# Two FFT convolution layers, twice: PSUM tiles that take any idle buffer, modal convolutions under the planner, mode rows loaded without a cast

## The chip, the cores and the metric

One core of a Trainium2 chip runs the whole program; the times are microseconds of that core. [...] The engines work on SBUF, on PSUM (eight banks, into which PE writes its products) and through DMA on the memory outside. Each engine takes its queue in order; semaphores hold an instruction until what it needs is there.

## The reference

Two layers alternate, twice, on a sequence of 2048 positions and 512 channels, in single precision:

```python
def _A_ref(q, k, v, shift_k, ssm_k, ssm_D):
    ...                                   # k_shift: causal convolution of k over 4 positions
    kv = k_shift * v
    kv_f, kf_f = rfft2(kv padded to 4096), rfft2(ssm_k padded to 4096)
    y = irfft2(kv_f * kf_f)[:, :S, :] + kv * ssm_D[None, None, :]
    return q * y

def _B_ref(u, log_A_real, A_imag, C_real, C_imag, log_dt, D_skip):
    A = -jnp.exp(log_A_real) + 1j * A_imag          # 128 modes for each channel
    C = (C_real + 1j * C_imag) * dt[:, None]
    P = jnp.exp((A * dt[:, None])[:, :, None] * pos[None, None, :])
    K = 2.0 * jnp.einsum("dn,dnl->dl", C, P).real   # 2048 taps from the modes
    y = irfft(rfft(u) * rfft(K))[:, :, :L] + u * D_skip
    return y

x = x + _A_ref(_layernorm(x), ...)
x = x + _B_ref(_layernorm(x), ...)
x = x + _A_ref(_layernorm(x), ...)
x = x + _B_ref(_layernorm(x), ...)
```

The convolution inside A and the taps K do not depend on `x`. So both are worked out once; the second A layer only scales a stored result.

## The kernel before

The program has four parts.

1. *Preparation.* The mode parameters are turned into logarithms and phases on 128 x 512 tiles. `split` (lines 627 to 634) writes each as a rounded value (a cast on ACT) and the rest (a subtraction, `hl[:, 1] = v - hl[:, 0]`, on the engine that it is given), and stores both to `rows_d`. Four tiles are split: `la` and `ai` on POOL, `ph` and `t2` on DVE.
2. *The long stage*, two streams that share the engines. `stream` builds the taps of layer B: `load_rows` (line 720) fetches the rows of a group of channels, `mags` multiplies them with tables (`pm`) and takes the exponential on ACT (`m`), `angles` puts phases into `pa`, rounds them on DVE (`y`) and subtracts the rounding by a second matmul into the same `pa`, `waves` takes sines on ACT, `products` multiplies on POOL (`xy`) and DVE (`e`), `contract` sums on PE (`pk`); there are 64 such steps, 4 for each of the 16 groups. When 4 groups are done, `spectrum_quarter` transforms their taps and stores the spectrum (`pc` to `spec`). `diagonal` works out the products of layer A (`kvt`, `prod`, `kv`), the spectrum of its kernel, the convolution of all four quarters of the channels, and updates `x`. A convolution is a chain: a forward transform in two steps (`pf`, then DVE transposes to `z`, then `pu`), products with the stored spectrum `kab` (`vv`, `sw`), an inverse transform in two steps (`pi`, a copy to `ie` by ACT, DVE transposes to `w`, then `po`), and `finish`.
3. *First modal round*: the normalization of `x`, and `conv_b(0)`. Here ACT writes the normalized `u` and copies `pu` into `sw`, POOL multiplies `sw` with `kab`, DVE writes `vv`.
4. *The scaling by the stored second A layer* (`gated_update`) and the *second modal round*, `conv_b(1)`, during which `x<-x,off` (`restore`, line 1085) puts back the mean on DVE.

*What sets the order.* Every operation goes through `Planner.record`. While `deferred` is false it is issued at once, in the order of the program (these rows bear line 177). While it is true, `flush` issues the operations in the order of `Planner.plan` (rows with line 342): a list schedule, which takes next the operation that can start first by given costs, with the order of recording between equals. In `plan` a tile is ready when the tile that was in its buffer has no reader left: `self.prior` gives each tile the one that many places earlier in its tag's rotation as there are buffers. Preparation, both modal rounds and the scaling are issued at once; only the long stage is planned, up to line 986. DVE and POOL exclude each other in the plan for operations with two SBUF inputs.

*PSUM.* During the long stage `f1` has two buffers of two banks, for `pf`, `pu`, `pi` and `pm`; `c1` has one bank for `kv` and `po`; `pa` has two banks and `pk` one. In the modal rounds `f1` has three buffers and `c1` two.

Of the kernel before, what the change touches and what calls it, by code (L numbers as in the profile page):

```python
# [102 lines left out]
class Op:  # L103
    def __init__(self, engine, n):
        self.engine, self.n, self.calls, self.uses, self.before, self.ordered = engine, n, [], [], set(), []
        self.ins = None


class Planner:
    RELEASE = {"V": 34, "S": 60, "G": 90, "T": 80, "D": 27}  # L110

    def __init__(self, tc, nc):
        self.tc, self.ops, self.tiles, self.deferred = tc, [], {}, False
# [106 lines left out]
    def prepare(self):  # L220
        ops = self.ops
        self.costs = [self.cost(op) for op in ops]
        self.follow = [[] for _ in ops]
# [5 lines left out]
        self.pending = [len(op.before) + len(op.ordered) for op in ops]  # L229
        names, self.prior, self.queue = {}, [], {}  # L230
        self.using, self.users = [], []
        for op in ops:
            l = []
            for t in op.uses:
                if t.tag_meta is None:
                    continue
                if t.name not in names:
                    names[t.name] = len(self.prior)
                    q = self.queue.setdefault(t.tag, [])
                    self.prior.append(q[-t.tag_meta.bufs] if len(q) >= t.tag_meta.bufs else None)  # L240
                    q.append(len(self.prior) - 1)
                    self.users.append(0)
                l.append(names[t.name])
                self.users[names[t.name]] += 1
            self.using.append(l)

    def plan(self, rank=None):
# [3 lines left out]
        idle, live = [0.0] * len(prior), [False] * len(prior)  # L251
        free = dict.fromkeys(self.engines, 0.0)
        ready = [0.0] * len(ops)
        start, end = [0.0] * len(ops), [0.0] * len(ops)
# [6 lines left out]
        for waiting in range(len(ops)):  # L261
            best = None
            for e, l in avail.items():
                pick = None
                base = free[e]
                if e == "D":
                    base = max(base, min(lanes))
                for n in l:
                    t = max(base, ready[n])
                    if e in "VG" and costs[n][2]:  # L270
                        t = max(t, lock["G" if e == "V" else "V"])
                    if pick is not None and (t, rank[n]) >= pick[:2]:
# [18 lines left out]
            op = ops[n]  # L291
            avail[e].remove(n)
            for u in using[n]:
                live[u] = True
            o, lat, extra = costs[n]
            start[n] = t
# [16 lines left out]
            if op.calls[0][0] == "dma_start":  # L313
                server = max(server, t + o) + extra
                end[n] = max(t + o + 1500, server + 1200)
                if e == "D":
                    lanes[lanes.index(min(lanes))] = end[n]
            elif e in "VG" and extra:
                lock[e] = t + o
            for u in using[n]:  # L320
                left[u] -= 1
                idle[u] = max(idle[u], end[n])
            for f, real in self.follow[n]:
                pending[f] -= 1
                ready[f] = max(ready[f], end[n] + self.RELEASE[ops[f].engine] if real else start[n] + o)
                if not pending[f]:
                    avail[ops[f].engine].append(f)
        self.length = max(end)
# [2 lines left out]
    def best(self):  # L331
        return self.plan()

    def flush(self):
        last = {}
        self.prepare()
        for n in self.best():
            op = self.ops[n]
            if op.ins is not None:
                continue  # L340
            for i, (name, a, k) in enumerate(op.calls):
                ins = getattr(self.engines[op.engine], name)(*a, **k).ins  # L342
# [11 lines left out]
def kernel(ctx: ExitStack, tc: tile.TileContext, out, x_in, kv_in, ssmk_in, ssmd_in,  # L354
                           la_in, ai_in, cr_in, ci_in, ldt_in, ldtb_in, dsk_in,
                           w1_in, w2_in, mm_in, w4_in, minus_in, tt_in, tg1_in, tg2_in, dbg=None):
    nc = tc.nc
    planner = Planner(tc, nc)
    V, S, G, T, Q = [planner.engine(e) for e in "VSGTD"]
    after = planner.after  # L360

# [497 lines left out]
    with ExitStack() as actx:  # L859
# [300 lines left out]
    G.tensor_sub(nbs[1], nb, nbs[1])  # L1160
    for _ in conv_b(1):
        pass


def run_steps(gens):
# [62 lines left out]
```

## Time and profile before

| | |
|---|---|
| median of 3 runs | 748.78 us (744.72 to 751.23) |
| the profiled execution | 749.08 us, of which the span from first to last instruction 747.2 us |
| busy: PE, DVE, ACT, POOL | 553.5, 508.5, 404.9, 350.1 us |
| transfers | 138.97 MB, 186 GB/s on average |

A timeline row gives the start, the length, the engine, the line, the operation, output <- inputs, the shapes and the count of instructions merged; in brackets stands the time for which the engine was idle before it and what ended that. A row of a stretch gives its bounds and length, the busy time of PE, PEld, DVE, ACT and POOL, PE's granted clock, the busy share of the transfer engines and GB/s.

### The profile page before, as it was taken

What the parts mean: (1) busy time and instruction counts of PE and PEld (TensorE: products, weight loads), DVE (VectorE), ACT (ScalarE), POOL (GpSimd) and SP (SyncE); (2) the same over time, 40 slices, a digit from 0 to 9 for tenths busy, and PEclk for the clock granted to TensorE, in tenths of its full rate; (3) what the DMA queues carried; (4) which work ended last, traced back from release to release, by engine and by line L of the source; (5) the groups of instructions that cost most, each with busy time, mean ns of one, the idle gap of its engine ahead of it and who ended that gap; (6) DMA issues with size and microseconds to landing.
All of it is one profiled execution on the core that took longest, in us unless ns stands there. A gap on an engine that the chain in (4) does not pass through costs nothing. (4 is left out here: it accounts for less than half of the span.)

```text
span 747.2 us, 20838 instructions
## 1 busy us (share of the span) xinstructions
PE 553.5 (74%) x8568; PEld 307.6 (41%) x8568; DVE 508.5 (68%) x918; ACT 404.9 (54%) x768; POOL 350.1 (47%) x342
## 2 busy tenths in 40 slices
PE   1649688896798888798778789344798871589984
PEld 0114334333334434664354366122465530255662
DVE  6924965547653456578978659664588879978863
ACT  4118518655539878749445386237473326746341
POOL 3618866967756745432353053500554520254551
PEclk9988979998989659698897979876899995899998
DMA  9499858694465315565676745679686712068764
GB/s 245 121 228 236 260 153 237 182 245 125 130 197 181 132 50 150 180 210 163 199 191 232 226 124 182 171 253 277 200 283 228 253 66 104 2 212 261 250 207 93
DMA packets 74499, 138.97 MB, mean 186 GB/s; under 512 B 8092, under 2 KB 37156, under 8 KB 72356
## 3 DMA queue, kind: packets, MB, share of 16 engines
q1 hardware_dynamic: 73540, 135.21, 60.7%
q0 software_dynamic: 864, 2.43, 0.9%
q8 instruction: 68, 1.11, 0.6%
q14 instruction: 27, 0.22, 0.1%
HBM read 97.75 MB, written 39.85 MB: 184 GB/s over the span
## 5 line engine op out<-in xcount | busy, mean ns | idle before, releaser
L342 POOL TENSOR_TENSOR xy<-tt,m 128x512 f32<-128x512 f32 x128 | 148.5, 1185 | 143.9 <-ACT tt L342 64.0
L177 POOL TENSOR_TENSOR sw<-sw,kab 128x512 f32<-128x512 f32 x64 | 80.6, 1280 | 119.3 <-ACT sw L177 112.1
L342 PE MATMUL kv<-prod,minus 128*128 128x512 f32 x128 | 80.3, 720 | 9.3 <-DVE prod L342 7.1
L342 POOL TENSOR_TENSOR prod<-kvt 128x512 f32<-128x512 f32 x64 | 79.8, 1269 | 15.6 <-DMA kv_d<-prod 9.7
L342 ACT ACTIVATE m<-pm 128x1024 f32<-128x1024 f32 x48 | 46.9, 1026 | 57.8 <-PE pm L342 55.9
L342 PE MATMUL pf<-kk,w 64*128 64x512 f32 x128 | 45.0, 755 | 39.9 <-DMA kk<-ssmk_in 21.0
L342 ACT ACTIVATE ab<-pa 128x512 f32<-128x512 f32 x64 | 38.3, 599 | 61.0 <-PE pa L342 61.0
L342 DVE TENSOR_TENSOR e<-pa,m 128x512 f32<-128x512 f32 x64 | 43.6, 681 | 31.5 <-ACT pa L342 25.3
L177 DVE TENSOR_TENSOR vv<-pu,kab 128x512 f32<-128x512 f32 x64 | 40.9, 677 | 35.0 <-ACT sw L177 32.5
L177 ACT COPY ie<-pi 128x1024 f32<-128x1024 f32 x32 | 32.4, 1013 | 58.7 <-PE pi L177 58.7
L342 DVE TENSOR_SCALAR y<-pa 128x512 fp32r<-128x512 f32 x64 | 43.5, 682 | 30.0 <-PE pa L342 29.5
L177 PE MATMUL pf<-u,w 64*128 64x512 f32 (+1 forms) x136 | 40.1, 681 | 25.8 <-ACT u L177 15.8
L342 DVE STREAM_TRANSPOSE zk<-pf 128x512 f32<-128x512 f32 x64 | 41.4, 688 | 25.1 <-PE pf L342 25.1
L177 PE MATMUL pi<-vv,mm 64*64 64x128 f32 x1024 | 53.4, 276 | 1.1 <-DVE vv L177 1.1
L177 PE MATMUL pi<-sw,mm 64*64 64x128 f32 x1024 | 52.3, 270 | 1.7 <-issue 1.7
L342 PE MATMUL pa<-tt,rw 64*128 64x512 f32 x64 | 35.2, 554 | 23.1 <-DVE e L342 23.0
L342 PE MATMUL pa<-y,minus 128*128 128x512 f32 x64 | 41.9, 660 | 10.1 <-DVE y L342 10.1
L342 PE MATMUL pk<-xy,e 128*32 128x64 f32 x2048 | 47.3, 240 | 2.9 <-POOL xy L342 1.5
L177 ACT COPY sw<-pu 128x1024 f32<-128x1024 f32 x32 | 32.3, 1013 | 30.7 <-PE pu L177 30.7
L177 PE MATMUL pu<-zu,w 64*64 64x128 f32 x1024 | 37.2, 281 | 14.3 <-DVE zu L177 12.2
L342 PEld LDWEIGHTS pk<-xy,e 128*32 128x32 f32 x2048 | 36.0, 121 | 28.6 <-issue 19.8
L342 PE MATMUL pu<-zk,w 64*64 64x128 f32 x1024 | 40.0, 301 | 9.3 <-DVE zk L342 6.6
(134 smaller groups left out, 1181.1 us busy)
## 6 DMA issues: line engine op xcount, KB each, us to landing
kab<-spec SPq DMA_DIRECT2D x94, 512.0 KB, 4.6
spec<-pc SPq DMA_DIRECT2D x64, 256.0 KB, 4.3
kvt<-kv_in SPq DMA_DIRECT2D x32, 312.0 KB, 5.0
kk<-ssmk_in SPq DMA_DIRECT2D x32, 128.0 KB, 5.7
xr<-x_in SPq DMA_DIRECT2D x8, 512.0 KB, 6.6
kv_d<-prod SPq DMA_DIRECT2D x16, 256.0 KB, 3.9
kdram<-ks SPq DMA_DIRECT2D x64, 64.0 KB, 2.2
kk<-kdram SPq DMA_DIRECT2D x32, 128.0 KB, 2.8
```

What stands on the lines that cost most here:

```text
L177: op.ins = getattr(self.engines[key], name)(*a, **k).ins
L342: ins = getattr(self.engines[op.engine], name)(*a, **k).ins
```

## The change

- In `plan`, tiles of the tags `c1` and `f1` of the long stage's PSUM pool (`shared`) have no place in a rotation: when an operation is chosen, its tile gets any buffer of the tag that is idle. `flush` moves the operands onto that buffer's first tile (so rows of the change show `pf` for all tiles of `f1`, and `kv` for all of `c1`). The tags of the modal rounds keep their rotation.
- The modal rounds and the scaling are planned too: the first flush comes after the first 16 steps of `conv_b(0)`, and a second one plans the rest. Since pools `xp` and `conv_q` lie where `conv_a` was, operations on them wait in the plan until all that use `conv_a` are done (`over`).
- `load_rows` loads straight into the matmul operand `rw`, four buffers instead of two and two; the cast goes.
- The second matmul of each `pm` is held in the plan until 600 ns ahead of the end of the last sine (`late`).
- The subtractions of `split(1, ...)` and `split(3, ...)` go to POOL.

```diff
 def prepare(self):
...
+                    pool = next((p for p in self.over if f"_{p}_" in t.tag), None)
+                    self.gate.append(self.over.get(pool))
                     q = self.queue.setdefault(t.tag, [])
-                    self.prior.append(q[-t.tag_meta.bufs] if len(q) >= t.tag_meta.bufs else None)
+                    ring = self.name(t) not in self.shared
+                    self.prior.append(q[-t.tag_meta.bufs] if ring and len(q) >= t.tag_meta.bufs else None)
+                    self.tag.append(None if ring else t.tag)
...
 def plan(self, rank=None):
...
                     for u in using[n]:
-                        if live[u] or prior[u] is None:
+                        if live[u]:
+                            continue
+                        if self.gate[u]:
+                            if rest[self.gate[u]]:
+                                ok = False
+                                break
+                            t = max(t, last[self.gate[u]] + self.RELEASE[e])
+                        tag = self.tag[u]
+                        if tag:
+                            if not open_[tag] or (self.FIFO and self.queue[tag][head[tag]] != u):
+                                ok = False
+                                break
+                            t = max(t, min(spare[tag][b] for b in open_[tag]) + self.RELEASE[e])
+                            continue
+                        if prior[u] is None:
                             continue
...
+                if tag and not live[u]:
+                    fit = [b for b in open_[tag] if spare[tag][b] + self.RELEASE[e] <= t + 1e-6]
+                    self.place[u] = max(fit, key=lambda b: (spare[tag][b], -b))
+                    open_[tag].remove(self.place[u])
...
+    planner.over = {"xp": "conv_a", "conv_q": "conv_a"}
+    planner.shared = {'c1_ps', 'f1_ps'}
...
-    split(1, ph, V)
-    split(3, t2, V)
+    split(1, ph, G)
+    split(3, t2, G)
...
-        raw = wk.tile([128, 2, 128], F32, name="raw", tag="raw", bufs=2)
+        rows[gi] = wk.tile([128, 2, 128], F32R, name="rw", tag="rw", bufs=4)
         q, g = divmod(gi, 4)
         for k in range(2):
-            Q.dma_start(raw[:, k, :], rows_d[k][q, :, g, :])
-        rows[gi] = wk.tile([128, 2, 128], F32R, name="rw", tag="rw", bufs=2)
-        V.tensor_copy(rows[gi], raw)
+            Q.dma_start(rows[gi].bitcast(F32)[:, k, :], rows_d[k][q, :, g, :])
...
-            T.matmul(pm[:, h], rows[gi][hs, 1, :], rhs, start=True, stop=True)
+            ins = T.matmul(pm[:, h], rows[gi][hs, 1, :], rhs, start=True, stop=True)
+            if last_sin[0] is not None and h:
+                ins.late.append((last_sin[0], 600))
...
         run_steps([(stream(), RT), (diag, RD)])
-        planner.flush()
...
     for _ in range(2 * NCH):
         next(first)
+    planner.flush()
     gctx.close()
     pctx.close()
+    planner.deferred = True
...
     for _ in conv_b(1):
         pass
+    planner.flush()
```

The order of the instructions changes on every engine. Three places follow; a row is one or more like instructions of an engine's queue.

PE, in the long stage, around the thirtieth of the 64 steps of the taps (`pa<-tt,rw` is its first matmul, `pa<-y,minus` the second, which needs DVE's `y`). Before:

```order
L342 MATMUL pu<-zk,w_108 64x128 x32
L342 MATMUL pk<-xy,e_625 32x64 x16
L342 MATMUL pa<-tt,rw 128x512
L342 MATMUL pa<-y,minus 128x512
L342 MATMUL pa<-tt,rw 128x512
L342 MATMUL pk<-xy,e_631 32x64 x16
L342 MATMUL pa<-y,minus 128x512
```

And in the change, at the same step:

```order
L411 MATMUL pk<-xy,e_616 32x64 x16
L411 MATMUL pa<-tt,rw 128x512
L411 MATMUL pf<-zk,w_108 64x128 x16
L411 MATMUL pa<-tt,rw 128x512
L411 MATMUL pk<-xy,e_622 32x64 x16
L411 MATMUL pa<-y,minus 128x512
L411 MATMUL pf<-kk,w_107 128x16x16x2 x2
```

The second matmul of the step stood directly behind the first; now 16 matmuls of another tile, a further first matmul and 16 of `pk` lie between. In the whole list the two stand side by side 9 times before and 3 times in the change. At the end of the stage both lists have the last `pk`, `pf`, `pu` and `po` in turn.

ACT, at the start of the first modal round (`u` is the normalized input, `sw` a copy of the transformed one). Before:

```order
L177 ACTIVATE u<-x,nb,rs 128x128 x40
L177 COPY sw<-pu 128x1024 x3
L177 COPY ie<-pi 128x64x16
L177 COPY sw<-pu 128x1024
L177 COPY ie<-pi 128x64x16
```

And in the change:

```order
L411 ACTIVATE u<-x,nb,rs 128x128 x31
L411 COPY sw<-pu 128x1024
L411 ACTIVATE u<-x,nb,rs 128x128 x6
L411 COPY sw<-pu 128x1024
L411 ACTIVATE u<-x,nb,rs 128x128 x3
L411 COPY sw<-pu 128x1024
L411 COPY ie<-pi 128x64x16
```

The first copy moved ahead of nine of the forty `u`, the second ahead of three. Over both rounds, in 7 of the 32 pairs of `vv` one half now stands ahead of ACT's copy of the same `pu`; before it was none.

DVE, at the start of the second modal round (`zu` are transposes of the first transform, `x<-x,off` puts back the mean). Before:

```order
L177 STREAM_TRANSPOSE zu<-pf 128x512 x4
L177 TENSOR_SCALAR x<-x,off 128x512 x4
L177 STREAM_TRANSPOSE zu<-pf 128x512 x2
L177 TENSOR_SCALAR x<-x,off 128x512 x4
L177 STREAM_TRANSPOSE zu<-pf 128x512 x2
L177 TENSOR_SCALAR x<-x,off 128x512 x8
L177 TENSOR_TENSOR vv<-pu,kab 128x512 x2
```

And in the change:

```order
L411 TENSOR_SCALAR x<-x,off 128x512 x4
L411 STREAM_TRANSPOSE zu<-pf 128x512 x8
L411 TENSOR_SCALAR x<-x,off 128x512
L411 STREAM_TRANSPOSE zu<-pf 128x512 x2
L411 TENSOR_SCALAR x<-x,off 128x512 x2
L411 TENSOR_TENSOR vv<-pu,kab 128x512 x2
L411 TENSOR_SCALAR x<-x,off 128x512 x2
L411 TENSOR_TENSOR vv<-pu,kab 128x512 x2
L411 STREAM_TRANSPOSE zu<-pf 128x512 x2
L411 TENSOR_SCALAR x<-x,off 128x512
L411 STREAM_TRANSPOSE zu<-pf 128x512 x2
L411 TENSOR_SCALAR x<-x,off 128x512
```

All sixteen `x<-x,off` stood ahead of the first `vv`; now seven do, and nine stand among the `vv` and `zu` behind it. On POOL the two subtractions `hl<-ph` and `hl<-t` stand directly behind `hl<-ai` and ahead of all `prod`; the 16 casts `rw<-raw` are gone from DVE.

More of the change, by code (lines that the diff above doesn't have):

```diff
@@ L222, in prepare @@
         self.costs = [self.cost(op) for op in ops]
+        for op in ops:
+            op.before = {o for o in op.before if ops[o.n:o.n + 1] == [o]}
+            op.ordered = [o for o in op.ordered if ops[o.n:o.n + 1] == [o]]
+            op.late = [(o, lead) for o, lead in op.late if ops[o.n:o.n + 1] == [o]]
         self.follow = [[] for _ in ops]
@@ L228, in prepare @@
                 self.follow[o.n].append((op.n, False))
-        self.pending = [len(op.before) + len(op.ordered) for op in ops]
+            for o, lead in op.late:
+                self.follow[o.n].append((op.n, lead))
+        self.pending = [len(op.before) + len(op.ordered) + len(op.late) for op in ops]
         names, self.prior, self.queue = {}, [], {}
-        self.using, self.users = [], []
+        self.using, self.users, self.gate, self.tag, self.handles, self.buffers = [], [], [], [], [], {}
+        self.held = {p: [] for p in self.over.values()}
         for op in ops:
@@ L245, in prepare @@
             self.using.append(l)
+            for p, h in self.held.items():
+                if any(f"_{p}_" in t.tag for t in op.uses if t.tag_meta is not None):
+                    h.append(op.n)
     def plan(self, rank=None):
@@ L251, in plan @@
         idle, live = [0.0] * len(prior), [False] * len(prior)
+        spare = {t: [0.0] * len(b) for t, b in self.buffers.items()}
+        open_ = {t: set(range(len(b))) for t, b in self.buffers.items()}
+        head = dict.fromkeys(spare, 0)
+        self.place = [None] * len(prior)
+        rest = {p: len(h) for p, h in self.held.items()}
+        last = dict.fromkeys(rest, 0.0)
+        holds = {p: set(h) for p, h in self.held.items()}
         free = dict.fromkeys(self.engines, 0.0)
@@ L319, in plan @@
                 lock[e] = t + o
+            for p, h in holds.items():
+                if n in h:
+                    rest[p] -= 1
+                    last[p] = max(last[p], end[n])
             for u in using[n]:
@@ L322, in plan @@
                 idle[u] = max(idle[u], end[n])
+                if not left[u] and self.tag[u]:
+                    spare[self.tag[u]][self.place[u]] = idle[u]
+                    open_[self.tag[u]].add(self.place[u])
             for f, real in self.follow[n]:
                 pending[f] -= 1
-                ready[f] = max(ready[f], end[n] + self.RELEASE[ops[f].engine] if real else start[n] + o)
+                ready[f] = max(ready[f], end[n] + self.RELEASE[ops[f].engine] if real is True else start[n] + o if real is False else end[n] - real)
                 if not pending[f]:
@@ L332, in best, with name, move @@
         return self.plan()
+    @staticmethod
+    def name(t):
+        return t.tag.rsplit("_", 1)[0]
+    def move(self, x):
+        to = self.where.get(x.tensor.name) if hasattr(x, "tensor") else None
+        if to is None:
+            return x
+        old, new = [int(np.prod(t.shape[1:])) for t in (x.tensor, to)]
+        dims = [list(d) for d in x.ap]
+        assert dims[0][0] == old and new >= old
+        return bass.AP(to, x.offset // old * new + x.offset % old, [[new, dims[0][1]]] + dims[1:])
     def flush(self):
@@ L336, in flush @@
         self.prepare()
-        for n in self.best():
+        order = self.best()
+        self.where = {self.handles[u].name: self.buffers[self.tag[u]][b] for u, b in enumerate(self.place)
+                      if b is not None and self.buffers[self.tag[u]][b].name != self.handles[u].name}
+        for n in order:
             op = self.ops[n]
@@ L341, in flush @@
             for i, (name, a, k) in enumerate(op.calls):
+                a, k = [self.move(x) for x in a], {n_: self.move(x) for n_, x in k.items()}
                 ins = getattr(self.engines[op.engine], name)(*a, **k).ins
```

10 lines of the change are left out of this document (8 added, 2 removed).

## The prediction

> **What bounds the kernel now.** I read the span cut into its stages first, then the idle time of PE inside the longest stage, and last the timeline of every DVE instruction that took far longer than its group.
>
> ```profile
> 53.30:475.00 421.70, 345.15 (x5040) 186.50 (x5040) 280.33 (x462) 264.12 (x534) 235.17 (x224) 0.87 0.63 182
> 512.00:615.00 103.00, 85.50 (x1664) 52.63 (x1664) 76.12 (x142) 51.59 (x82) 42.74 (x34) 0.95 0.62 211
> 642.00:747.00 105.00, 82.80 (x1672) 52.64 (x1672) 74.82 (x117) 49.25 (x76) 45.97 (x41) 0.94 0.59 182
> ```
>
> The stage rows give the window, its length, then PE, PEld, DVE, ACT and POOL busy, the granted clock, and DMA. From the first `pm` matmul (53.3) to the last taps (475), PE works 345.15 of 421.70 us and idles 76.55. The two modal rounds (512 to 615, 642 to 747) leave PE 17.5 and 22.2 us idle, most of it filling and draining. So the kernel is a PE queue with holes, and an edit pays where it closes a hole. The largest single holes lie in the first two stages, and have one cause:
>
> ```profile
> L342 DVE CAST rw<-raw 128x256 fp32r<-128x256 f32 x16 | 29.7, 1854 | 5.2 <-DMA raw<-rows_d 5.2
> 85.36 9.56 DVE L342 CAST rw<-raw 128x256 fp32r<-128x256 f32 x1
> 92.30 2.47 POOL L342 TENSOR_TENSOR prod<-kvt 128x512 f32<-128x512 f32 x2
> 95.67 0.76 PE L342 MATMUL pa<-tt,rw 64*128 64x512 f32 x1 [7.55 <-DVE e L342]
> 174.37 7.02 DVE L342 CAST rw<-raw 128x256 fp32r<-128x256 f32 x1
> 178.95 2.29 POOL L342 TENSOR_TENSOR xy<-tt,m 128x512 f32<-128x512 f32 x2
> 182.77 1.56 PE L342 MATMUL pu<-zk,w 64*64 64x128 f32 x24 [6.10 <-DVE zk L342]
> 198.25 6.70 DVE L342 CAST rw<-raw 128x256 fp32r<-128x256 f32 x1
> 202.33 2.47 POOL L342 TENSOR_TENSOR prod<-kvt 128x512 f32<-128x512 f32 x2
> 205.70 2.02 PE L342 MATMUL kv<-prod,minus 128*128 128x512 f32 x2 [4.94 <-DVE prod L342]
> 236.73 0.32 DVE L342 CAST rw<-raw 128x256 fp32r<-128x256 f32 x1
> ```
>
> A cast of 128x256 takes 0.32 us at 236.73, but three of the sixteen took 9.56, 7.02 and 6.70. Each ended (94.92, 181.39, 204.95) about 0.15 us after POOL's products ended (94.77, 181.24, 204.80). So a DVE copy or subtraction between SBUF tiles can stand still while POOL's two-input products follow each other, and goes on when POOL pauses; DVE's queue stands behind it, and PE idles 7.55, 6.10 and 4.94 us for what is queued there. [...]
>
> **Term 1, the start.** The same happens before the stream begins:
>
> ```profile
> 18.50 1.26 POOL L177 TENSOR_TENSOR hl<-ai,hl 128x512 fp32r<-128x512 f32 x1 [6.86 <-ACT hl L177]
> 19.92 13.93 SPq L177 DMA_DIRECT2D rows_d<-hl  x3
> 22.07 0.61 ACT L177 CAST hl<-t 128x512 fp32r<-128x512 f32 x1
> 22.19 10.35 DVE L177 TENSOR_TENSOR hl<-ph,hl 128x512 fp32r<-128x512 f32 x1 [0.69 <-ACT hl L177]
> 24.63 7.36 POOL L342 TENSOR_TENSOR prod<-kvt 128x512 f32<-128x512 f32 x6
> 32.46 0.73 DVE L177 TENSOR_TENSOR hl<-t,hl 128x512 fp32r<-128x512 f32 x1
> 44.38 2.17 PE L342 MATMUL pf<-kk,w 64*128 64x512 f32 x4 [7.00 <-DMA kk<-ssmk_in]
> 25.00:30.00 5.00, 4.11 (x8) 1.18 (x6) 5.00 (x1) 0.00 (x0) 5.00 (x5) 1.00 0.25 101
> 30.00:35.00 5.00, 2.73 (x6) 1.02 (x8) 5.00 (x6) 0.00 (x0) 2.65 (x3) 1.00 0.15 25
> ```
>
> `hl<-ph` stands 10.35 us behind POOL's six products, so the two subtractions end at 33.19. SP's queue waits with their stores (13.93 us for three issues), and every load queued behind them waits too: in 25 to 35 the transfer engines are busy 0.25 and 0.15 (the column before the last). The change puts both subtractions on POOL, directly behind `hl<-ai` and ahead of the products. The last input is there at 22.68 (22.07 + 0.61), and two subtractions at 1.26 end at about 24.7: SP goes on 8.5 us earlier. Since the transfers are what it then feeds, I bound the gain by the transfer time lost, 5 x 0.75 + 5 x 0.85 = 8.0 us. POOL's products start 2.5 us later; PE waits 7.00 us for `kk` afterwards, which covers that, and without that cover 2.5 us would come off. I take **7**, between 0 and 8.
>
> **Term 2, the casts.** Sixteen casts go and no instruction replaces them, since the DMA writes `rw` itself: two loads for each of the 16 groups, as before, now four buffers ahead instead of two, so a load can only be issued earlier. What the three stalls cost is read from the windows around them:
>
> ```profile
> 85.40:95.00 9.60, 2.72 (x8) 0.79 (x7) 9.60 (x3) 3.04 (x9) 9.60 (x10) 0.90 0.79 241
> 174.40:181.40 7.00, 2.27 (x7) 0.63 (x7) 7.00 (x3) 4.50 (x12) 6.84 (x6) 1.00 0.01 2
> 198.20:205.00 6.80, 2.56 (x38) 1.17 (x36) 6.80 (x3) 2.38 (x6) 6.80 (x8) 1.00 0.16 54
> 70.00:85.00 15.00, 13.45 (x211) 7.21 (x210) 10.25 (x21) 11.21 (x30) 12.88 (x12) 0.91 0.81 230
> 95.00:110.00 15.00, 13.10 (x89) 5.37 (x90) 9.90 (x20) 2.85 (x4) 9.30 (x10) 0.72 0.58 158
> ```
>
> PE idles 6.88 + 4.73 + 4.24 = 15.85 us in the three. The rest of the stage idles (76.55 - 15.85) / (421.70 - 23.40) = 0.152 of its time, which would be 3.55 us in 23.40. So 12.3 us are lost to the stalls. PE does not make them up: it is busy 13.45 of 15 us ahead of the first stall and 13.10 behind it. The other thirteen casts (29.7 - 23.28 = 6.4 us together) lie on an engine that idles a third of the stage. I take **12.3**; bounds 0 (all made up later) and 25 (29.7 less 16 x 0.3, all of it on the path).
>
> **Term 3, the order of the long stage.** With PSUM tiles that take any idle buffer the planner may pass a tile that is not ready. Its trace is the pair `pa<-tt,rw`, `pa<-y`: the second needs DVE's `y` of the first.
>
> ```profile
> L342 PE MATMUL pa<-y,minus 128*128 128x512 f32 x64 | 41.9, 660 | 10.1 <-DVE y L342 10.1
> 245.94 0.50 PE L342 MATMUL pa<-y,minus 128*128 128x512 f32 x1 [1.32 <-DVE y L342]
> ```
>
> Where they stand side by side PE waits (1.32 us at 245.94, where nothing stands between). In PE's order they stand side by side 9 times of 64 now and 3 times in the change. Of the 10.1 us, 6/9 would be 6.7. I take **4**, because PE isn't the only engine in this loop; the bounds are 10 either way, since nothing in the trace excludes that the freer order opens as much wait elsewhere.
>
> **Term 4, the first modal round.** ACT normalizes `u` and copies `sw`; now all 40 `u` go ahead of the first copy.
>
> ```profile
> 512.34 12.41 ACT L177 ACTIVATE u<-x,nb,rs 128x128 f32<-128x128 f32 x32 [0.35 <-DMA x<-x_d]
> 519.96 1.11 PE L177 MATMUL pu<-zu,w 64*64 64x128 f32 x32 [1.50 <-DVE zu L177]
> 524.66 1.90 ACT L177 COPY sw<-pu 128x1024 f32<-128x1024 f32 x2
> 527.12 2.08 PE L177 MATMUL pf<-u,w 64*128 64x512 f32 x4 [3.95 <-DVE vv L177]
> ```
>
> In the change 31 stand ahead. The 23 of them in this row end at 512.34 + 23 x 0.388 = 521.3, when `pu` (521.07) is just ready: the first copy comes 3.4 us earlier, and PE's 3.95 us wait behind it shrinks. I take **3**, between 0 and 4.
>
> **Term 5, the second modal round.** Here sixteen subtractions `x<-x,off` on DVE stand ahead of the first `vv` now.
>
> ```profile
> L177 DVE TENSOR_SCALAR x<-x,off 128x512 f32<-128x512 f32 x16 | 6.5, 471 | 0.0
> 640.50 11.26 ACT L177 ACTIVATE u<-x,nb,rs 128x128 f32<-128x128 f32 x29 [0.75 <-DVE nb L177]
> 644.77 2.51 DVE L177 STREAM_TRANSPOSE zu<-pf 128x512 f32<-128x512 f32 x4 [1.14 <-PE pf L177]
> 652.98 1.98 PE L177 MATMUL pu<-zu,w 64*64 64x128 f32 x32 [5.62 <-DVE zu L177]
> 655.02 1.01 ACT L177 COPY sw<-pu 128x1024 f32<-128x1024 f32 x1 [3.25 <-PE pu L177]
> 656.11 2.52 POOL L177 TENSOR_TENSOR sw<-sw,kab 128x512 f32<-128x512 f32 x2 [11.11 <-ACT sw L177]
> ```
>
> In the change four go ahead of the transposes, while DVE waits for PE anyway; eight transposes at 0.63 from about 645.3 end at 650.4, `pu` at about 652.6, and ACT is free at 651.76: the copy comes 2.4 us earlier. But nine of the sixteen now stand behind the first `vv`, in five groups (two, one, one, two, three), when POOL multiplies `sw`. They go from SBUF to SBUF, as the casts did; whether they are caught as those were no row shows, since POOL idles beside them now (11.11 us ahead of 656.11). The row of the casts gives the nearest price: 25.2 us over 16 is 1.6 a cast, with POOL busy 235.17 of 421.70; POOL is busy 45.97 of 105 here, so 1.25 a group, 6.2 in all, and DVE is busy 74.82 of 105, so 4.4 on the path (bounds 0 and 5 x 2.52 = 12.6). The net is **-2**. [...]
>
> Besides, in 7 of the 32 pairs of both rounds one half of `vv` reads `pu` ahead of ACT's copy, which delays that copy by one `vv`. I take 0, with bounds of 5 either way.
>
> **The sum.** 7 + 12.3 + 4 + 3 - 2 = 24.3 us. The profiled execution took 749.08 (span 747.2), close to the median of 748.78. The forecast is 749.08 - 24.3 = 724.8, so **724.5** for the median.
>
> **Rivals.** *The stalls are made up anyway.* If POOL's products and ACT's queue limit the long stage, what is gained at the stalls is lost again, and only terms 1 and 4, at half, stay: 5 us, 744. For it: POOL and ACT work on during a stall (9.60 and 3.04 of 9.60). Against it: POOL is busy only 235 of 421.70. *The planner gives up what it gains.* Filling any idle `f1` buffer favours whichever stream is ready, and one stream may end late; if term 3 falls to its lower bound, 749.08 - 24.3 + 14 = 739. Against it: in PE's order both streams still end side by side. *Slower: the stall moves.* POOL's products stay, and where the new order places such DVE instructions among them (the nine `x<-x,off`, and some six small ones of the normalizers), each that is caught costs what a caught cast cost, 23.28 / 3 = 7.8 us. From four on the gain is gone; five give 749 - 24 + 39 = 764. Three of sixteen casts were caught; POOL's products in the second round come in pairs of 2.52 us, with pauses, which speaks against five.
>
> **Chances.** The forecast 0.64, with 704 to 741; the planner's loss 0.14 (739); made up anyway 0.12 (744); slower 0.10. A measurement of this kernel tells about 1% from no change, 7.5 us. Faster by over 1% holds the forecast and the planner's loss, 0.78; within 1%, 0.12; slower, 0.10. The range is 704 (terms at 8, 23, 10 and 4, term 5 at 0) to 745 (the first rival).
>
> **What would show it.** No DVE instruction over 3 us between 20 and 450; `hl<-ph` on POOL at about 1.26 us; the first `pm` near 46 instead of 53.3; the 32 `u` that start at 512.34 now near 489; fewer than 5 us under `pa<-y <-DVE y`; the first `sw` copy about 12 us behind the first `u` in round one. I am wrong if PE's idle time between the first `pm` and the last taps stays above 70 us, or if `x<-x,off` averages over 2 us.

## The result, and the profile after

The changed kernel took 709.13 us (median of four runs, 700.53 to 713.34) against 749.76 before: a ratio of 0.943, 95% interval 0.933 to 0.953. That is 40.6 us less where 24.3 were forecast; the time lies inside the range given. Run again beside other kernels it took 709.57, ratio 0.949 (0.945 to 0.953). Ratios leave out the runs that lie more than 1.5% above the fastest of the same kernel; medians are over all runs.

The first rows to set side by side are those of the page: span, PE's busy time, and the granted clock by slices. In the rows PE does the matrix products and PEld loads their weights, DVE and POOL do the vector work, ACT activation functions, casts and copies; SPq rows are transfers that SP issues. After:

```profile
span 706.2 us, 20796 instructions
PE 536.0 (76%) x8568; PEld 297.8 (42%) x8568; DVE 473.4 (67%) x900; ACT 405.4 (57%) x768; POOL 352.7 (50%) x344
PEclk9999998999998696999899898759999965999998
```

Before:

```profile
PE 553.5 (74%) x8568; PEld 307.6 (41%) x8568; DVE 508.5 (68%) x918; ACT 404.9 (54%) x768; POOL 350.1 (47%) x342
PEclk9988979998989659698897979876899995899998
```

PE executes the same 8568 matmuls, yet is busy 17.5 us less; its idle time (span less busy) fell from 193.7 to 170.2, by 23.5. The forecast of 24.3 us was a sum of idle times; its total is near the fall in idle time, and beside it stands a saving of 17.5 us of which it held nothing. The clock rows say where to look: of the slices of 5 to 7 tenths in the long stage, six before, two are left.

The stages of the kernel after (window, its length, then PE, PEld, DVE, ACT, POOL busy, granted clock, DMA share, GB/s): the long stage from the first magnitude matmul to the last `pk`, the tail, round one, the scaling, round two.

```profile
43.95:435.51 391.56, 332.44 (x5046) 178.79 (x5046) 251.47 (x448) 264.97 (x534) 234.61 (x223) 0.91 0.67 198
435.51:471.33 35.82, 10.43 (x145) 5.21 (x145) 18.85 (x62) 10.85 (x21) 5.49 (x7) 0.68 0.73 232
471.33:575.97 104.64, 85.47 (x1664) 52.48 (x1664) 76.56 (x141) 51.35 (x82) 42.76 (x34) 0.93 0.60 208
575.97:604.23 28.26, 8.47 (x18) 3.57 (x17) 26.17 (x99) 17.72 (x39) 3.31 (x8) 0.64 0.24 82
604.23:706.20 101.97, 83.26 (x1673) 53.37 (x1672) 77.38 (x116) 49.17 (x76) 45.17 (x38) 0.94 0.60 188
```

The long stage of before, cut at the same instructions:

```profile
53.32:473.91 420.59, 345.15 (x5040) 186.47 (x5040) 279.23 (x460) 264.12 (x534) 235.17 (x224) 0.87 0.63 182
```

With the same marks before (53.32, 473.91, 512.04, 614.37, 641.86, end 747.2) the change is: start 9.4 us earlier, long stage 29.0 shorter, tail 2.3 shorter, round one 2.3 longer, scaling 0.8 longer, round two 3.4 shorter; together 41.0. In the long stage PE idles 16.3 us less (75.4 to 59.1) and is busy 12.7 less. Busy time times clock hardly moves: 345.15 x 0.87 = 300 before, 332.44 x 0.91 = 303 after. The work is the same; it was done at a higher clock. That is not a matter of two single runs: over 35 runs beside the experiments the kernel before had a mean clock of 0.871 (0.858 to 0.888), the changed one over ten 0.900 (0.893 to 0.907).

### The profile page after: what moved, and what is told of

Its sections match the earlier page's. It is cut to its first block, busy times and chain, and to the rows that moved or that the text cites. A ratio compares the mean times of both kernels' runs of the same rounds, so it can differ in the third digit from the quotient of the medians.

```text
span 706.2 us, 20796 instructions
## 1 busy us (share of the span) xinstructions
PE 536.0 (76%) x8568; PEld 297.8 (42%) x8568; DVE 473.4 (67%) x900; ACT 405.4 (57%) x768; POOL 352.7 (50%) x344
## 5 line engine op out<-in xcount | busy, mean ns | idle before, releaser
L411 PE MATMUL pf<-u,w 64*128 64x512 f32 (+1 forms) x200 | 60.1, 693 | 28.6 <-ACT u L411 15.9
L411 PE MATMUL kv<-prod,minus 128*128 128x512 f32 x128 | 75.9, 684 | 2.9 <-POOL prod L411 2.0
L411 ACT ACTIVATE m<-pf 128x1024 f32<-128x1024 f32 x48 | 47.7, 1024 | 44.0 <-PE pf L411 42.5
L411 DVE STREAM_TRANSPOSE zu<-pf 128x512 f32<-128x512 f32 x96 | 63.2, 692 | 12.4 <-PE pf L411 12.4
L411 DVE TENSOR_TENSOR vv<-pu,kab 128x512 f32<-128x512 f32 x64 | 42.8, 678 | 24.6 <-ACT sw L411 20.0
L411 PE MATMUL pk<-xy,e 128*32 128x64 f32 x2048 | 45.7, 234 | 5.1 <-POOL xy L411 3.6
L411 ACT COPY pc<-pf 128x512 f32<-128x512 f32 x64 | 35.6, 585 | 22.9 <-DMA spec<-pc 13.8
L411 PE MATMUL po<-w,w 128*64 128x512 f32 x128 | 36.8, 675 | 11.6 <-DVE w L411 11.5
L411 ACT ACTIVATE u<-x,nb,rs 128x128 f32<-128x128 f32 x101 | 40.8, 482 | 6.4 <-DMA x<-x_d 5.3
```

## The clock behind a hole

What a stall of DVE did to PE's clock can be read around the longest cast of before (85.36 to 94.92), in stretches of 5 us:

```profile
85.00:90.00 5.00, 3.12 (x9) 0.79 (x7) 5.00 (x2) 2.93 (x9) 5.00 (x6) 1.00 0.97 255
90.00:95.00 5.00, 0.00 (x0) 0.00 (x0) 5.00 (x2) 0.51 (x2) 5.00 (x6) 0.81 0.62 222
95.00:100.00 5.00, 3.30 (x27) 1.34 (x30) 4.11 (x7) 0.00 (x0) 0.03 (x1) 0.50 0.28 87
100.00:105.00 5.00, 4.80 (x58) 2.39 (x51) 2.86 (x8) 1.93 (x4) 4.27 (x5) 0.67 0.58 146
105.00:110.00 5.00, 5.00 (x17) 1.64 (x16) 2.93 (x5) 0.92 (x1) 5.00 (x5) 1.00 0.89 240
180.00:190.00 10.00, 7.23 (x73) 3.87 (x74) 5.65 (x8) 2.56 (x7) 1.25 (x2) 0.66 0.60 182
200.00:210.00 10.00, 5.06 (x35) 2.31 (x27) 8.07 (x6) 2.83 (x7) 6.26 (x8) 0.79 0.34 98
```

And in the timeline of PE, where the same pair of matmuls stands ahead of the hole, behind it, and later:

```profile
86.76 1.12 PE L342 MATMUL kv<-prod,minus 128*128 128x512 f32 x2
97.47 2.05 PE L342 MATMUL kv<-prod,minus 128*128 128x512 f32 x2 [1.03 <-DVE prod L342]
104.69 1.02 PE L342 MATMUL kv<-prod,minus 128*128 128x512 f32 x2
```

PE stood still in 90 to 95; afterwards the granted clock is 0.50, then 0.67, and the pair takes 2.05 us instead of 1.12. Behind the other two stalls the clock is 0.66 and 0.79. A PE that is busy 4.80 of 5 us at a clock of 0.67 looks like a PE that catches up. Here the clock is half behind a stand of 7.55 us (up to the matmul at 95.67), and 1.00 again in 105 to 110. Shorter waits are followed by it too. In the kernel with three stalls, below, PE waits 2.52 us up to 76.94; the pair of `kv` at 77.53 then takes 2.06 us (1.13 at 71.31), and the clock is 0.50 from 80 to 85. In the changed kernel it is 0.50 from 87.5 to 90, behind a wait of 1.77 us up to 86.33. How long a wait it takes is not settled here.

## The experiments

The gains below are (1 - ratio) x 748.6 us, the median of the kernel before beside the middle group of runs; each ratio is taken against runs of the kernel before on the same chip.

| kernel | ratio (95%) | gain, us |
|---|---|---|
| before + subtractions on POOL | 0.990 (0.986 to 0.995) | 7.3 |
| before + rows loaded without a cast | 0.972 (0.966 to 0.977) | 21.1 |
| before + both | 0.957 (0.951 to 0.963) | 32.0 |
| changed, casts and DVE subtractions put back | 0.975 (0.968 to 0.982) | 18.6 |
| changed, again | 0.949 (0.945 to 0.953) | 38.3 |
| changed, all PSUM tags in rotation | 0.956 (0.951 to 0.960) | 33.2 |
| changed, second `pm` not held | 0.943 (0.938 to 0.948) | 42.7 |
| changed, rounds issued in program order | 0.949 (0.944 to 0.955) | 38.1 |
| changed, three stalls put in | 0.979 (0.971 to 0.988) | 15.5 |
| changed, only round one in program order | 0.942 (0.937 to 0.947) | 43.6 |
| changed, row stores on POOL's queue | 0.941 (0.935 to 0.946) | 44.5 |
| changed, the last two together | 0.936 (0.929 to 0.943) | 47.8 |

### The two subtractions alone

```diff
-    split(1, ph, V)
-    split(3, t2, V)
+    split(1, ph, G)
+    split(3, t2, G)
```

> The kernel before with one edit: the two subtractions of the mode rows (ph and t2) go to POOL. Both theories: the first magnitude matmul comes about 9 us earlier (at 44 instead of 53.3), and the time falls by 7 to 9 us, to about 741. The casts remain, so three or so of them still last over 5 us. If the gain at the start is made up later, 749.

Measured 740.99 us: a gain of 7.3 us (3.9 to 10.6), as forecast (7). In its timeline the first magnitude matmul comes 5.2 us earlier than before, not the 9 that were expected, and two casts are still caught:

```profile
48.14 0.73 PE L342 MATMUL pm<-tg,rw 64*128 64x512 f32 x4 [3.37 <-issue]
158.96 7.25 DVE L342 CAST rw<-raw 128x256 fp32r<-128x256 f32 x1
182.27 6.73 DVE L342 CAST rw<-raw 128x256 fp32r<-128x256 f32 x1
```

### The casts alone, and both

```diff
-        raw = wk.tile([128, 2, 128], F32, name="raw", tag="raw", bufs=2)
+        rows[gi] = wk.tile([128, 2, 128], F32R, name="rw", tag="rw", bufs=4)
...
-            Q.dma_start(raw[:, k, :], rows_d[k][q, :, g, :])
-        rows[gi] = wk.tile([128, 2, 128], F32R, name="rw", tag="rw", bufs=2)
-        V.tensor_copy(rows[gi], raw)
+            Q.dma_start(rows[gi].bitcast(F32)[:, k, :], rows_d[k][q, :, g, :])
```

> The kernel before with one edit: the mode rows are loaded straight into the operand, four buffers, no cast. Theory A (the stalled casts cost the idle time of PE beside them and also a lower granted clock behind each hole): idle time of the long stage falls by about 12 us and PE's busy time there by about 8 with the mean clock rising from 0.877 to about 0.89, total about 729. Theory B (the freer PSUM order gives what was more than forecast): idle time falls by 12 at the most, the clock stays near 0.877, total 737 or more.

> The kernel before with both of these edits, planner as before. Theory A: nearly all of the change's gain, about 715, clock about 0.895. Theory B: about 728, clock below 0.885.

The casts alone gave 728.03 us, a gain of 21.1 (16.9 to 25.3); both gave 716.03, a gain of 32.0 (27.5 to 36.6). Some four fifths of the change's gain lie in two small edits. The planner's part adds 6 us to them by the run again and 11 by the first result; with an uncertainty of 5 us and more it is only just clear of nothing. The long stages, of the casts alone and of both:

```profile
51.69:457.23 405.54, 341.61 (x5042) 185.91 (x5042) 254.13 (x449) 264.85 (x534) 234.91 (x224) 0.88 0.67 191
```

```profile
45.69:444.34 398.65, 339.19 (x5046) 184.16 (x5046) 252.59 (x447) 265.31 (x534) 234.76 (x223) 0.89 0.68 194
```

Without the casts PE idles 63.9 us here instead of 75.4, which is 11.5 less where 12.3 were forecast; its busy time falls by 3.5. The two together make 15.0 of the 20.7 by which the spans differ (747.2 and 726.5); most of the rest lies ahead of the stage (1.6 us) and in the tail (3.3 us shorter). With both edits idle time falls by 16.0 and busy time by 6.0. Over all runs the mean clock was 0.871 for the kernel before, 0.884 without the casts and 0.891 with both. So theory A held in the total. In the profile of the first step less of it is clock than it said (3.5 us, not 8), but how much is open: the two profiled runs, at clocks of 0.877 and 0.879, lie nearer to each other than the means do. PE's busy time multiplied by the mean clock is 478 to 487 us in all fourteen profiles, so that 0.871, 0.884 and 0.891 stand for some 554, 546 and 542 us of busy time (an estimate), a saving of 8 and then 12 us.

### The planner's part alone

The two diffs above are undone in the changed kernel:

```diff
-    split(1, ph, G)
-    split(3, t2, G)
+    split(1, ph, V)
+    split(3, t2, V)
...
+        rows[gi] = wk.tile([128, 2, 128], F32R, name="rw", tag="rw", bufs=2)
+        V.tensor_copy(rows[gi], raw)
```

> The changed kernel with the casts put back on DVE (two and two buffers) and the two subtractions back on DVE; the planner's part of the change alone is left. Theory A: casts of 5 to 10 us come back, total 740 to 749, clock about 0.88. Theory B: total about 733, clock about 0.895, because the freer order fills the holes.

Measured 731.11 us, a gain of 18.6 (13.3 to 24.0). Theory A had said 740 to 749 and is wrong there; theory B's 733 is near. In the timeline of DVE:

```profile
88.22 7.08 DVE L411 CAST rw<-raw 128x256 fp32r<-128x256 f32 x1
139.98 7.69 DVE L411 CAST rw<-raw 128x256 fp32r<-128x256 f32 x1
```

Two casts are caught for 14.8 us together, where three stood 23.3 us before. Not the same ones: the fourth of the sixteen is caught in both, the seventh and eighth no longer (0.57 and 0.28 us), and the sixth now is. The single gains (7.3, 21.1 and 18.6, in sum 47.0) come to more than 40, though the excess is within their intervals. The planner's part is worth about 18 us on top of the stalls and some 6 to 11 without them.

### What in the planner's part gains

The changed kernel ran again beside three others, each with one edit. The first keeps the rotation of all PSUM tags:

```diff
-    planner.shared = {'c1_ps', 'f1_ps'}
+    planner.shared = set()
```

The second doesn't hold the second `pm`:

```diff
-            if last_sin[0] is not None and h:
-                ins.late.append((last_sin[0], 600))
```

The third issues both rounds and the scaling at once, as before:

```diff
         run_steps([(stream(), RT), (diag, RD)])
+        planner.flush()
...
-    planner.flush()
     gctx.close()
     pctx.close()
-    planner.deferred = True
```

> The changed kernel as it is, beside the next three on the same chip: 709 (between 700 and 713), clock 0.90.

> The changed kernel with one edit: all PSUM tags keep their rotation (no tag is shared); the modal rounds stay planned and the second magnitude matmul stays held. If the free choice of a buffer is what the planner's part gains, the long stage goes back to that of the kernel with both fixes and the planner of before (398.7 us, clock 0.89) and the time rises by 6 to 8 us, to about 716. If the held matmul is the source, the time stays within 3 us of the changed kernel.

> The changed kernel with one edit: the second matmul of each pm is not held in the plan. If the free choice of buffers is the source of the planner's gain, the time stays within 3 us of the changed kernel. If the hold is the source, it rises by 6 to 8 us, the long stage to about 398 us.

> The changed kernel with one edit: both modal rounds are issued in the order of the program again, as before. By the prediction's terms 4 and 5 (+3 and -2) it would be 1 us slower than the changed kernel. By the profiles so far (233.9 us from the first u matmul to the end with unplanned rounds, 234.9 with planned ones) it is 1 us faster; round one takes 102 instead of 104.6 us, and the gap and round two take 132 instead of 130. More than 4 us either way would be a surprise.

Measured 709.57, 714.26, 707.50 and 711.60 us. The free choice of a buffer is worth about 5 us (38.3 against 33.2; the intervals of the ratios overlap a little, 0.945 to 0.953 and 0.951 to 0.960). The hold is worth nothing that can be seen, the planning of the rounds as a whole neither. (In the profiled run of the kernel with both rounds at once, round two took 110.2 us, where the kernel before took 105.3 with the same order; that is not explained.) The long stage with rotation:

```profile
43.21:439.35 396.14, 332.42 (x5046) 181.67 (x5046) 254.80 (x449) 264.17 (x534) 235.18 (x224) 0.91 0.68 196
```

And three groups of the same kernel in that stage (busy time, mean, and the idle time of PE ahead of it with what ended it); `pm` is the first magnitude matmul, `pi<-vv` the first step of the inverse transform:

```profile
L411 PE MATMUL pa<-tt,rw 64*128 64x512 f32 x64 | 33.4, 522 | 15.2 <-DVE e L411 15.1
L411 PE MATMUL pi<-vv,mm 64*64 64x128 f32 x512 | 30.1, 302 | 13.8 <-DVE vv L411 12.5 <-DVE zu L411 1.0 <-DVE zk L411 0.3
L411 PE MATMUL pm<-tg,rw 64*128 64x512 f32 x96 | 25.0, 528 | 9.6 <-ACT m L411 5.5 <-DMA rw<-rows_d 1.7 <-issue 1.2
```

In the changed kernel, where rows show `pf` for both `pm` and `pi`, the same three and the second matmul of the steps:

```profile
L411 PE MATMUL pa<-tt,rw 64*128 64x512 f32 x64 | 33.0, 518 | 11.1 <-DVE e L411 8.7 <-DVE mv L411 2.2 <-DMA rw<-rows_d 0.2
L411 PE MATMUL pf<-vv,mm 64*64 64x128 f32 x512 | 29.0, 296 | 1.4 <-DVE vv L411 0.6 <-issue 0.4 <-DVE zk L411 0.3
L411 PE MATMUL pf<-tg,rw 64*128 64x512 f32 x96 | 27.1, 567 | 18.2 <-ACT m L411 10.1 <-ACT pc L411 3.3 <-DVE zk L411 2.7
L411 PE MATMUL pa<-y,minus 128*128 128x512 f32 x64 | 37.2, 581 | 8.8 <-DVE y L411 7.7 <-DMA kdram<-ks 1.0
```

PE idles 63.7 us against 59.1 in the changed kernel, at the same clock. The 4.6 us are what is left of larger moves both ways: the free choice takes 12.4 us off the wait under `pi<-vv` and 4.1 off that under `pa<-tt`, and the first magnitude matmul waits 8.6 more.

Against the kernel before with both fixes the account is another one. There PE idles 59.5 us in the long stage (398.65 less 339.19), as much as in the changed kernel. What the planner's part takes off the stage beside the two fixes, 7.1 us in these two profiles, is almost all busy time (339.2 to 332.4), at clocks of 0.89 and 0.91. Why its order leaves PE a higher clock at equal idle time, these runs don't show. Here is `pa<-tt` of that kernel:

```profile
L342 PE MATMUL pa<-tt,rw 64*128 64x512 f32 x64 | 34.5, 539 | 13.7 <-DVE e L342 13.5 <-DMA rw<-rows_d 0.2
```

Of the 12 us by which this wait shrank from before (23.1) to the change (11.1), 9.4 are there already without the planner's part. And `pa<-y`, the wait that the prediction chose, is 10.1 us for `y` before, 8.0 with both fixes and 7.7 in the change, though the pairs that stand side by side fell from 9 to 3.

### A stall that has nothing to do with POOL

Three sums that keep DVE busy for about 7.6 us each go into the changed kernel, unknown to the plan; nothing reads their result.

```diff
+        if name == "tensor_reduce":
+            return 400, 485, False
...
+        if (gi, k) in ((1, 2), (5, 0), (6, 0)):
...
+            after(V.tensor_reduce(junk, ones[:, None].to_broadcast([128, 56, 128]), axis=mybir.AxisListType.XY, op=ALU.add), ie)
```

> The changed kernel with three stalls put into DVE's queue that have nothing to do with POOL: a sum over 56 x 128 values (about 7.5 us) directly behind e of the steps (1,2), (5,0) and (6,0), which the planner takes for 0.4 us. If a stall costs only the share that the prediction's second term gave it (12.3 us of PE idle for 23.3 us of stalls, 0.53), 709.5 + 22.5 x 0.53 = 721, with the clock at 0.90. If PE's holes also lower the granted clock and put the streams out of step, as the kernels with and without the casts suggest (20.8 us for 23.3), about 730, the clock at 0.885 or below, and PE's busy time in the long stage up by 5 us or more.

```profile
79.02 7.59 DVE L413 TENSOR_REDUCE junk<-ones 128x1 f32<-128x7168 f32 x1
```

```profile
42.59:455.40 412.81, 338.50 (x5046) 182.23 (x5046) 274.21 (x453) 264.94 (x534) 234.79 (x223) 0.88 0.64 187
80.00:85.00 5.00, 3.33 (x35) 1.34 (x34) 5.00 (x1) 0.59 (x1) 3.96 (x5) 0.50 0.49 159
85.00:90.00 5.00, 0.95 (x2) 0.52 (x2) 4.94 (x11) 0.07 (x1) 1.69 (x4) 0.50 0.00 0
90.00:95.00 5.00, 5.00 (x39) 1.90 (x39) 2.70 (x4) 2.70 (x7) 2.31 (x2) 0.54 0.77 236
```

Its ratio of 0.979 is 22.8 us above that of the changed kernel (38.3 less 15.5; by the two intervals 16 to 30): 22.8 us of stalls cost about their own length, not the 12 of the prediction's rate. (The ratio rests on two of its four runs; the median of all four, 738.91, lies 29 us above 709.57.) In the long stage idle time rises from 59.1 to 74.3. Busy time rises from 332.4 to 338.5, at a clock of 0.88; that alone proves little, since equal orders differ by as much (below), but over all runs the mean clock is 0.881 (0.873 to 0.890) against 0.900 (0.893 to 0.907). The rows of the first stall show it only in part: the clock was down before it, behind a wait of 2.52 us for `ks`, and stood at 0.50 to 90 and 0.54 from 90 to 95. Behind the second and third it was 0.91 (185 to 195) and 0.86 (225 to 235). So a stall in which POOL has no part has this price: about 15 us more idle time for 22.8, and a lower mean clock (0.881 against 0.900).

### A version that beats both

The first edit issues round one at once, as before, and plans only the scaling and round two (the flush moves as in the third kernel above); the second lets POOL issue the four stores of the mode rows behind its own subtractions; a third kernel has both.

```diff
     for _ in first:
         pass
+    planner.deferred = True
```

```diff
-        Q.dma_start(rows_d[k].rearrange(...)
+        G.dma_start(rows_d[k].rearrange(...)
```

> The changed kernel with one edit: the first modal round is issued in the order of the program as before, the scaling and the second round stay planned. By the profiles so far round one falls from 104.6 to about 101.5 and the rest stays at 130.2: 3 us less than the changed kernel, about 706. If the wait that the planned order opens in round one is an accident of one run, 709.

> The changed kernel with one edit: the four stores of the split mode rows are issued by POOL, behind its own subtractions, not by SP, whose queue stood 5.5 us behind three of them. If SP's wait still holds back the start, the first magnitude matmul comes 2 to 4 us earlier than 43.9 and the time falls to about 706. If the transfers were the limit there (busy 0.84 of the time), nothing changes: 709.

> The changed kernel with both of these edits: 703 if both gains stand and add, 709 if neither does.

Measured 704.04, 705.26 and 702.77 us. With both, the interval (0.929 to 0.943) lies wholly below that of the changed kernel run again (0.945 to 0.953): about 1.3% faster. Against the first measurement of the changed kernel (0.933 to 0.953) it is not clear. The first edit's gain stands where it was expected, in round one. These are the long stage and round one of the kernel with both rounds in program order, and then of the one with round one alone:

```profile
43.84:435.63 391.79, 333.70 (x5046) 180.33 (x5046) 251.66 (x448) 264.38 (x534) 234.55 (x223) 0.91 0.68 197
472.20:573.45 101.25, 85.28 (x1664) 52.43 (x1664) 75.99 (x141) 51.69 (x82) 42.83 (x34) 0.95 0.63 212
```

```profile
44.62:441.78 397.16, 339.51 (x5046) 183.76 (x5046) 251.63 (x448) 264.81 (x534) 234.79 (x223) 0.89 0.67 195
478.05:579.60 101.55, 85.43 (x1664) 52.55 (x1664) 75.89 (x141) 51.73 (x82) 42.74 (x34) 0.95 0.61 212
```

Round one takes 101.3 and 101.6 us at once and 104.6 planned. All fourteen profiles bear this out in PE's idle time. In round one it is 15.3 to 16.8 us where the round is issued at once (seven profiles) and 18.8 to 22.1 where it is planned (seven). In round two it is the other way: 20.4 to 25.4 at once (five), 17.4 to 19.7 planned (nine). That fits the times: planning both gains nothing that can be seen, and planning round two alone does.

These two kernels also have the same order on PE, DVE and ACT throughout the long stage. Its idle time is the same (58.1 and 57.7 us) and its length differs by 5.4 us: the clock alone, 0.91 and 0.89, moves one run of this kernel against another by that much.

The second edit's expectation failed in its place. SP no longer stands behind the stores, but the first magnitude matmul came at 44.64, not earlier. The long stage took 384.5 us there, and 385.1 in the kernel with both edits, instead of 391.6; the total fell by 4 to 6 us, with intervals that just overlap. Why the stage is shorter, these runs don't settle.

## Why the prediction was right or wrong

**The cause and the sign held; the sum came out in part by luck.** The casts (6.70 to 9.56 us) and the subtractions (the first 10.35 us) caught behind POOL's products were the largest holes, and without them some four fifths of the gain came. By stages, PE's idle time fell by 5.6 us ahead of the long stage, 16.3 in it and 1.6 in the tail, rose by 2.3 in round one, and fell by 2.4 in the scaling and round two; the forecast had 7, 16.3, 0, a fall of 3 and a rise of 2. So terms 4 and 5 both had the wrong sign and cancel, and the 16.3 come without term 3 (16.0 with both fixes alone). No DVE instruction of the kind lasts over 3 us between 20 and 450 (a row of 3.15 us is sixteen statistics merged).

**Term 1, 7 us: right.** 7.3 us alone (3.9 to 10.6). The subtractions run on POOL at 1.26 us, and SP's queue waits 5.5 us instead of 13.9; the first magnitude matmul stands at 43.95, where about 46 was forecast (48.14 with the subtractions alone, so the rest of the change brings it forward too):

```profile
21.09 5.53 SPq L178 DMA_DIRECT2D rows_d<-hl  x3
23.54 1.26 POOL L178 TENSOR_TENSOR hl<-ph,hl 128x512 fp32r<-128x512 f32 x1 [2.48 <-ACT hl L178]
43.95 0.50 PE L411 MATMUL pf<-tg,rw 64*128 64x512 f32 x2 [1.10 <-DMA rw<-rows_d]
```

**Term 2, 12.3 us: right mechanism, too small.** 21.1 measured. The step that failed is "PE does not make them up: it is busy 13.45 of 15 us ahead of the first stall and 13.10 behind it". Both rows bear a clock, 0.91 and 0.72, and I read past it. Busy time times clock is 12.2 us of work ahead and 9.4 behind: 2.8 us of work lost, 3.4 at the pace of the row ahead. If the other two stalls are alike, 10 more, 22.6 in all. That is an estimate from one stall, and that it comes so near to 21.1 is in part luck: in the profile without casts 11.5 us of idle time and 3.5 of busy time leave the long stage, and 4.9 of the 20.7 lie ahead of it and in the tail. The put-in stalls show a price of the same size from the other side (22.8 for 22.8 us, 16 to 30).

**Term 3, 4 us: near in size, by luck, and the wrong wait.** Against rotation the free choice of a buffer gains about 5 us, above all under `pi<-vv`. The term forecast less idle time in the long stage; beside the two fixes the planner's part brings none (59.5 and 59.1 us), but less busy time. The sign "fewer than 5 us under `pa<-y`" failed (7.7); counting neighbours in PE's order did not measure that wait.

**Term 4, +3 us: wrong sign.** The first copy of `sw` does come 9.3 us behind the first matmul of round one instead of 12.6, and the wait behind it that the term named shrinks (`pf<-u` for `vv`, 3.9 to 1.5 us). But what is late next takes it back. POOL waits for the spectrum of the third pair, and ACT's copies wait for `vv` that stand ahead of them:

```profile
494.57 1.27 POOL L411 TENSOR_TENSOR sw<-sw,kab 128x512 f32<-128x512 f32 x1 [4.68 <-DMA kab<-spec]
497.34 1.01 ACT L411 COPY sw<-pu 128x1024 f32<-128x1024 f32 x1 [2.64 <-DVE vv L411]
```

In the groups of round one, ACT's and PE's, after and then before:

```profile
L411 ACT COPY sw<-pu 128x1024 f32<-128x1024 f32 x16 | 16.1, 1009 | 17.1 <-PE pu L411 11.7 <-DVE vv L411 5.4
L411 PE MATMUL po<-w,w 128*64 128x512 f32 x64 | 18.9, 680 | 7.0 <-DVE w L411 6.9
```

```profile
L177 ACT COPY sw<-pu 128x1024 f32<-128x1024 f32 x16 | 16.1, 1012 | 14.8 <-PE pu L177 14.8
L177 PE MATMUL po<-w,w 128*64 128x512 f32 x64 | 17.4, 617 | 3.1 <-DVE w L177 3.0
```

The 5.4 us behind `vv` are what I had set at 0 with bounds of 5. Round one is 2.3 us longer instead of 3 shorter, and issuing it at once gave that back in all seven profiles; which of the two waits costs more was not tried apart.

**Term 5, -2 us: wrong sign.** Scaling and round two are 2.6 us shorter. The restores cost 2.9 us more than before, not 6.2:

```profile
L411 DVE TENSOR_SCALAR x<-x,off 128x512 f32<-128x512 f32 x16 | 9.4, 623 | 2.7 <-ACT u L411 2.7
```

And in the timelines of POOL and DVE:

```profile
617.62 6.63 POOL L411 TENSOR_TENSOR sw<-sw,kab 128x512 f32<-128x512 f32 x5 [11.78 <-ACT sw L411]
618.77 1.90 DVE L411 TENSOR_SCALAR x<-x,off 128x512 f32<-128x512 f32 x2
623.01 1.51 DVE L411 TENSOR_SCALAR x<-x,off 128x512 f32<-128x512 f32 x1
```

Five products of POOL follow each other from 617.62 to 624.25. The two restores that start at 618.77 were through at 620.67, in the middle of that run; the one at 623.01 took 1.51 us, where the mean before was 0.47. So a restore waited about 1 us, less than one product (6.63 / 5 = 1.33), not for the whole run. The slower rival, in which each would cost 7.8 us, fell with this.

**The rivals.** "The stalls are made up anyway" (744) and "the planner gives up what it gains" (739) are refuted by the kernels with the two fixes, with and without the rest (716 and 709). Terms 3 to 5 add to 5 in the forecast; the planner's part measured 6 to 11 on top of the fixes, but not where these terms had it. So of the 16 us that the forecast lacked, 9 are term 2's. About 4 appear where the two fixes meet (32.0 together against 28.4 apart), and as many are the planner's beyond 5, with a mean clock of 0.900 against 0.891; both are within the intervals of the ratios, so neither is shown.

## What to carry to other kernels

Weigh PE's busy time by the granted clock before you say that an engine has caught up behind a hole; here stalls of DVE cost about their own length (22.8 us for 22.8, by the intervals 16 to 30), some two thirds of it as idle time (15.2 us) and part of the rest as a lower clock (0.881 against 0.900). A short instruction between SBUF tiles on DVE can be dear beside long runs of POOL's products: three of sixteen casts took 6.70 to 9.56 us here, where the one at 236.73 took 0.32. First look for a way not to need it (a load straight into the operand, 21.1 us here), then for another engine (7.3 us). A planner that prices each instruction by its shape doesn't see such stalls, and a copy that it puts ahead only helps if what is needed next is early too. One profile of each kernel can't tell a difference of some us in a stage that PE fills, since the clock moves equal orders by that much (391.8 us at 0.91 and 397.2 at 0.89); a stage's idle time repeated far better here (58.1 and 57.7 us).

## What the hardware showed that I had not expected

A hole of 7.55 us in PE's work, up to 95.67 in the kernel before, was followed by a granted clock of 0.50 until 102.5 and 0.83 until 105, and a pair of matmuls in it took 2.05 us instead of 1.12: what another engine held up shows here as more PE busy time. Of the 41 us of the profiled difference 17.5 are busy time; the two fixes have some 12 of them by the mean clocks, and why the rest comes with the planner's order is open. Equal orders of instructions ran the long stage in 391.8 and 397.2 us, with 58 us of idle time in both. And DVE behind POOL's products waits in two ways: casts for 6.70 to 9.56 us, while six to ten instructions of POOL ran, restores for about 1 us; what decides between them stays open.
